# Output sums grown beside their own step's first-matmul turns, with the weights loaded uncast in quarters

## The chip, the cores and the metric

One core of one Trainium2 chip. The metric is the device time of one execution in microseconds (us). All times of a kernel here are the median of its runs. The span of a profile runs from the first to the last instruction and is about 1.7 us shorter than the device time of the same execution. The granted clock is the share of full speed at which TensorE was clocked, as the profile records it.

## The reference, cut to what matters

A short convolution along the sequence with one softmaxed 7-tap filter per head, then a dense block with a Swish of learned slope:

```python
w = softmax(weight)                       # 8 heads x 7 taps
out[b, s, h, :] = sum_k w[h, k] * x_pad[b, s + k, h, :]      # x: 8 x 4096 x 192
h = out.reshape(32768, 192) @ w_in        # 192 -> 2048
g = h / (1 + exp(-beta * h))
return g @ w_out                          # 2048 -> 192, float32
```

## The kernel before

The kernel works in 33 steps: two of 256 tokens, then 31 of 512, each for two halves of the batch at once (rows 0 to 63 and 64 to 127 of the partitions). A step has 16 turns, one for each 128 columns of `w_in`. In a turn TensorE makes the first matmuls (`hidden`), ScalarE turns them into `g`, and TensorE adds to the output sums (`output`) of **the step before**; VectorE copies finished sums out of PSUM (an eviction). "A pair" below is two output matmuls of 192 columns that run together on the two row halves. The convolution of step s+2 is made by VectorE during step s, seven taps in three groups, 21 instructions; for the first two steps TensorE makes it with diagonal matrices.

```python
def hidden(s, fc):
    ...
    ph = psum_h.tile([128, 2, TOK], FP32, name="ph")
    for j in range(NG):                                  # 3
        for h in range(2):                               # the two row halves
            nc.tensor.matmul(ph[:, h, 0:n], w_in_s[rows, j, cols], cts[s][rows, j, 0:n], ...)
    nc.scalar.activation(gs[s][:, fc, :, 0:n], ph[:, :, 0:n], AF.Silu, scale=beta[:, fc : fc + 1])

def output(s, u):                                        # called with s - 1: one step behind
    nb = steps[s][2] // BLK
    per = 2 * nb                                         # 8 pairs a turn in a full step
    for i in range(u * per, (u + 1) * per):
        blk, fc = divmod(i, NF)                          # one block of 128 tokens at a time
        ...
```

The loads. The first chunk (`x0`) has the queue of SyncE to itself. GpSimd's queue, which casts while it loads, brings the first quarter of `w_in`, **then the second chunk (`x1b`)**, then the rest. Only 64 rows of `w_in` are loaded; VectorE copies them to the other 64.

```python
load_x(nc.sync, x0, 0, NB)
...
load_w_in(0)                        # gpsimd, float32 -> bfloat16 in the DMA
for h in range(2):
    nc.gpsimd.dma_start(out=x1b[:, :, h, :], in_=x_v[0, TOK : 2 * TOK, h, :]...)
for i in range(1, NW):
    load_w_in(i)
... # then w_out_raw in four parts, scaled by 1/beta on GpSimd
def copy_w_in(i):
    nc.vector.tensor_copy(w_in_s[DG : 2 * DG, :, cols], w_in_s[0:DG, :, cols])
```

In step 0 the rest of the set-up is hung between the turns. On TensorE it stands in program order, so a late operand stops all that follows (the profile after shows it: 1.6 and 2.9 us):

```python
first_work = {
    0: lambda: (first_xt(), taps()),
    2: lambda: (more(xt1_work)(), copy_w_in(1)),   # transposes of the second chunk
    4: lambda: (more(xt1_work)(), copy_w_in(2)),
    6: lambda: (more(conv1_work)(), copy_w_in(3)), # convolution of step 1 on TensorE
    8: more(conv1_work),
    11: more(conv1_work),
}
```

## Time and profile before

| | before |
|---|---|
| device time, median of 4 runs | 696.3 us |
| span of the profile | 695.1 us |
| TensorE busy | 687.6 us, 99% |
| first first-matmul of step 0 | 10.9 us |
| first full-width activation (start of step 2) | 37.2 us |
| granted clock over the span | 1.000 |

First the head of the profile page: the span, and busy time with its share, engine by engine (PE is TensorE, DVE VectorE, ACT ScalarE, POOL GpSimd).

```profile
span 695.1 us, 24865 instructions
...
PE 687.6 (99%) x11467; PEld 526.6 (76%) x11467; DVE 551.4 (79%) x938; ACT 580.0 (83%) x546; POOL 70.0 (10%) x83
```

TensorE is the bound. Now its timeline near the end (start, length, engine, line, operation, output and inputs, shapes, count). L395 is the first matmuls, L442 the output sums:

```profile
676.21 0.83 PE L395 MATMUL ph<-ct,w_in_s 64*128 64x512 bf16 x6
...
677.51 0.83 PE L395 MATMUL ph<-ct,w_in_s 64*128 64x512 bf16 x6
...
678.82 0.83 PE L395 MATMUL ph<-ct,w_in_s 64*128 64x512 bf16 x6
```

A turn is 1.31 us, with no wait named. The Trainium skill, page "TensorE: Matmul & The Clock Gate", section "Wait — 56ns, not 53.3ns?", gives N/2.4 + 2.5 ns for a matmul of N columns at full clock; the estimate from it for this stream is 3 x (512/2.4 + 2.5) + 8 x (192/2.4 + 2.5) = 1307 ns, and the trace agrees. Only the start and the end can move.

The table of stretches for 12 to 28 us, in step 0 and the beginning of step 1. Columns: the stretch, its length, busy time of TensorE, its weight loads, VectorE, ScalarE and GpSimd, each with a count, then the granted clock, the DMA share and GB/s.

```profile
core 0: us, PE busy (x) PEld busy (x) DVE busy (x) ACT busy (x) POOL busy (x), PEclk, DMA share, GB/s
12.00:16.00 4.00, 3.93 (x70) 2.94 (x65) 2.27 (x6) 3.02 (x5) 0.94 (x1) 1.00 1.09 277
16.00:20.00 4.00, 3.86 (x42) 2.77 (x40) 3.94 (x4) 2.68 (x5) 3.78 (x3) 1.00 1.71 239
20.00:24.00 4.00, 3.09 (x41) 2.30 (x37) 4.00 (x5) 2.91 (x5) 4.00 (x4) 1.00 0.57 57
24.00:28.00 4.00, 3.73 (x74) 3.28 (x71) 4.00 (x7) 3.98 (x7) 4.00 (x6) 1.00 2.03 180
```

The timelines of single engines in the same part: GpSimd's issue of the second chunk (L176), TensorE at its transposes (L243 with `x1b`), VectorE's copies of the last two weight quarters (L172) and the beginning of the convolution for step 2 (L376), and ScalarE's first full-width activations (L402).

```profile
3.72 1.66 POOL L176 DMA_DIRECT2D x1b<-in_x_dram  x2
```

```profile
12.95 0.83 PE L395 MATMUL ph<-ct,w_in_s 64*128 64x256 bf16 x12
13.71 0.47 PE L243 MATMUL po<-ident_b,x1b 128*64 128x128 bf16 x10
```

```profile
16.80 3.04 DVE L172 COPY w_in_s<-w_in_s 64x1536 bf16<-64x1536 bf16 x2
19.88 2.65 DVE L376 TENSOR_SCALAR ct<-xt,cw 128x512 bf16<-128x512 bf16 x2
```

```profile
37.18 18.64 ACT L402 ACTIVATE g<-ph,beta 128x1024 bf16<-128x1024 f32 x18 [1.02 <-PE ph L395]
```

The second chunk is issued at 3.7 us, was there when TensorE came to it at 13.7, and step 2 begins at 37.2. In brackets stands idle time and what ended it.

### The profile page before, as it was taken

How to read it: one execution, taken by the hardware profiler on the slowest of the kernel's cores; microseconds unless marked ns; L12 is line 12 of the kernel's file. 1: busy time of each engine (PE TensorE's matmuls, PEld its weight loads, DVE VectorE, ACT ScalarE, POOL GpSimd, SP SyncE). 2: the span in 40 equal slices, each digit the busy share in tenths (PEclk: the TensorE clock that was granted, in tenths of full speed). 3: DMA queues.
4: the chain of work that ended last, by engine and by line, in shares of the span. 5: the costliest groups of instructions: out<-in, count | busy, mean ns of one | idle time of the engine just before them, and what ended most of it. 6: DMA issues, size and time to landing. Idle time of an engine off the chain costs nothing.

```text
span 695.1 us, 24865 instructions
## 1 busy us (share of the span) xinstructions
PE 687.6 (99%) x11467; PEld 526.6 (76%) x11467; DVE 551.4 (79%) x938; ACT 580.0 (83%) x546; POOL 70.0 (10%) x83
## 2 busy tenths in 40 slices
PE   9999999999999999999999999999999999999997
PEld 6867777777777777777777777777777777777777
DVE  5999998998777987777987777987778987777222
ACT  6898888888888888888888888888888888888881
POOL 7934455000000000000000000000000000000000
PEclk9999999999999999999999999999999999999999
DMA  9999999922232022222023222032222122211012
GB/s 193 144 159 159 168 177 171 123 63 70 54 65 71 27 68 72 47 70 70 26 71 70 49 70 70 25 71 70 48 71 55 40 70 71 48 48 48 25 48 70
DMA packets 181497, 54.57 MB, mean 79 GB/s; under 512 B 146432, under 2 KB 181072, under 8 KB 181392
## 3 DMA queue, kind: packets, MB, share of 16 engines
q0 software_dynamic: 98048, 14.89, 29.8%
q1 hardware_dynamic: 83296, 38.09, 23.9%
q8 instruction: 89, 1.46, 0.9%
q14 instruction: 16, 0.13, 0.1%
q10 hardware_dynamic: 48, 0.01, 0.0%
HBM read 28.98 MB, written 37.29 MB: 95 GB/s over the span
## 4 chain that ended last, share of the span: by engine, by line
PE 96%; DVE 3%; ACT 0%; issue 0%
PE po L442 48%; PE ph L395 46%; DVE ct L378 2%; PE ph L256 0%; DVE w_in_s L172 0%; DVE ct L376 0%; PE ph L205 0%; PE po L209 0%; PE po L243 0%; ACT g L402 0%; PE po L256 0%; DVE xt L346 0%; DVE osb L457 0%; DVE ct L327 0%; ACT xt_145 L269 0%
## 5 line engine op out<-in xcount | busy, mean ns | idle before, releaser
L402 ACT ACTIVATE g<-ph,beta 128x1024 bf16<-128x1024 f32 (+1 forms) x528 | 572.7, 1090 | 96.7 <-PE ph L395 92.6
L442 PEld LDWEIGHTS <-g 64*128 64x128 bf16 x8192 | 369.2, 94 | 101.9
L442 PE MATMUL po<-w_out_s,g 64*128 64x192 bf16 x8192 | 429.8, 243 | 0.0
L395 PE MATMUL ph<-ct,w_in_s 64*128 64x512 bf16 (+1 forms) x3168 | 426.2, 370 | 2.0 <-ACT g L402 1.1
L378 DVE SCALAR_TENSOR_TENSOR ct<-xt,cw,ct 128x512 bf16<-128x512 bf16 x558 | 379.4, 745 | 0.0
L395 PEld LDWEIGHTS <-w_in_s 64*128 64x128 bf16 x3168 | 162.5, 94 | 56.4 <-issue 2.9
L456 DVE COPY osb<-po 128x384 f32<-128x384 f32 x127 | 70.8, 558 | 126.9 <-PE po L442 120.7
L457 DVE TENSOR_TENSOR osb<-po,osb 128x384 f32<-128x384 f32 x129 | 71.5, 555 | 6.0 <-ACT osb L454 1.6
L95 POOL DMA_DIRECT2D xd<-in_x_dram x60 | 54.4, 909 | 46.1 <-DMA xd<-in_x_dram 42.3
L376 DVE TENSOR_SCALAR ct<-xt,cw 128x512 bf16<-128x512 bf16 x93 | 29.5, 372 | 0.0
L454 ACT COPY osb<-po 128x192 f32<-128x192 f32 x2 | 0.6, 320 | 9.9 <-PE po L442 9.9
L352 POOL TENSOR_TENSOR w_out_s<-w_out_raw,beta_r 128x768 bf16<-128x768 f32 x4 | 6.2, 1568 | 2.5 <-DMA w_out_raw<-in_moe_w_out_dram 2.5
L205 PE MATMUL ph<-zeros 128*128 128x512 bf16 x7 | 3.5, 623 | 1.3 <-DVE warm L129 1.3
L172 DVE COPY w_in_s<-w_in_s 64x1536 bf16<-64x1536 bf16 x4 | 4.4, 1121 | 0.1
L256 PE MATMUL po<-xt_145,diag 128*128 128x256 f32 x28 | 4.4, 296 | 0.0
L256 PEld LDWEIGHTS po<-xt_145,diag 128*128 128x128 f32 x28 | 3.6, 189 | 0.7 <-issue 0.6
L256 PEld LDWEIGHTS ph<-xt_145,diag 128*128 128x128 f32 x14 | 3.1, 327 | 0.6 <-ACT xt_145 L269 0.6
L256 PE MATMUL ph<-xt_145,diag 128*128 128x256 f32 x14 | 3.4, 427 | 0.1
L185 POOL DMA_DIRECT2D w_out_raw<-in_moe_w_out_dram x4 | 3.1, 771 | 0.3 <-DMA x1b<-in_x_dram 0.3
L295 ACT ACTIVATE ct<-po,rn 128x256 bf16<-128x256 f32 x1 | 0.5, 475 | 2.6 <-PE po L256 2.6
L165 POOL DMA_DIRECT2D w_in_s<-in_moe_w_in_dram x4 | 2.7, 669 | 0.0
L205 PEld LDWEIGHTS <-zeros 128*128 128x128 bf16 x7 | 0.8, 126 | 2.3 <-DVE warm L129 1.3
(51 smaller groups left out, 28.1 us busy)
## 6 DMA issues: line engine op xcount, KB each, us to landing
out_dram<-osb SPq DMA_DIRECT2D x60, 384.0 KB, 3.1
xd<-in_x_dram POOLq DMA_DIRECT2D x54, 198.0 KB, 14.5
w_out_raw<-in_moe_w_out_dram POOLq DMA_DIRECT2D x4, 384.0 KB, 9.4
out_dram<-osb SPq DMA_DIRECT2D x7, 192.0 KB, 3.7
xd<-in_x_dram POOLq DMA_DIRECT2D x6, 192.0 KB, 13.7
x_83<-in_x_dram SPq DMA_DIRECT2D x4, 192.0 KB, 2.9
w_in_s<-in_moe_w_in_dram POOLq DMA_DIRECT2D x4, 192.0 KB, 7.7
xt<-xd SPq DMA_TRANSPOSE x30, 5.1
```

The source lines that it names most:

```text
L95: nc.gpsimd.dma_start(out=xd[r0:, :, h, :], in_=x_v[p, t0:t1, h, :].rearrange("t (c d) -> t c d", c=NG),)
L172: nc.vector.tensor_copy(w_in_s[DG : 2 * DG, :, cols], w_in_s[0:DG, :, cols])
L205: nc.tensor.matmul(pf[:, 0, :], zeros[:, 0:128], zeros, start=True, stop=True)
L256: nc.tensor.matmul(pv, diag[:, c, k, :], xt0[:, c, o : o + n], start=(k == 0), stop=(k == K - 1),)
L352: nc.gpsimd.tensor_tensor(w_out_s[:, c0 : c0 + n, :], w_out_raw[:, c0 : c0 + n, :], beta_r[:, c0 : c0 + n].unsqueeze(2).to_broadcast((128, ...
L376: nc.vector.tensor_scalar_mul(dst, src, scalar)
L378: nc.vector.scalar_tensor_tensor(out=dst, in0=src, scalar=scalar, in1=dst, op0=ALU.mult, op1=ALU.add)
L395: nc.tensor.matmul(ph[:, h, 0:n], w_in_s[rows, j, cols], cts[s][rows, j, 0:n], start=(j == 0), stop=(j == NG - 1),)
L402: nc.scalar.activation(gs[s][:, fc, :, 0:n], ph[:, :, 0:n], AF.Silu, scale=beta[:, fc : fc + 1])
L442: nc.tensor.matmul(po[:, r, b * D : (b + 1) * D], g[rows, fc, h, q * BLK : (q + 1) * BLK], w_out_s[rows, fc, :], start=(fc == 0), stop=(fc ...
L456: nc.vector.tensor_copy(dst, po[:, 0, cols])
L457: nc.vector.tensor_tensor(dst, po[:, 1, cols], dst, ALU.add)
```

## The change

Intent: let the output sums of a step begin two turns behind its own first matmuls, so that the early steps, in which ScalarE sets the pace and TensorE has room, take some of the output work; the lag then grows over steps 0 to 4. Two blocks of 128 tokens are summed in turn in one PSUM tile. And load all weights as they are (32 bit, by the plain DMA queue), in quarters, to be cast and crossed by GpSimd and VectorE. The core of the diff, cuts marked:

```diff
-    psum_o = ... bufs=2
+    psum_a = ... bufs=1 ;  psum_b = ... bufs=1
 ...
-    load_x(nc.sync, x0, 0, NB)
+    for b in range(HB):
+        load_x0(b)                  # all on nc.sync
+    load_w_in(0)
+    load_w_out(0)
+    for b in range(HB, NB):
+        load_x0(b)
+    for i in range(1, NW):
+        load_w_in(i)
+        load_w_out(i)
 ...
+    cross_w_in(0)                   # VectorE: 2 copies of 64 x 768, 32 bit -> 16
+    cast_w_in(0)                    # GpSimd: waits for the DMA
+    for h in range(2):
+        load_x1(h)                  # GpSimd: the second chunk
+    scale_w_out(0)
+    for i in range(1, NW):
+        cast_w_in(i)
+        scale_w_out(i)
 ...
+    class Job: ...                  # two blocks, 32 pairs, in slot "a" or "b"
+        def ready(self, s, u):
+            fcs = NF if self.s < s else max(0, u - LAG + 1)
+            return self.done < fcs * self.nb
 ...
-        0: lambda: (first_xt(), taps()),
-        2: lambda: (more(xt1_work)(), copy_w_in(1)),
-        4: lambda: (more(xt1_work)(), copy_w_in(2)),
-        6: lambda: (more(conv1_work)(), copy_w_in(3)),
+        0: lambda: (first_xt(), cross_w_in(1)),
+        2: more(xt1_work),
+        3: lambda: cross_w_in(2),
+        4: more(xt1_work),
+        6: more(conv1_work),
+        7: lambda: cross_w_in(3),
 ...
-    pops = {1: 12, 2: 26}
+    quota = {0: 2, 1: 4, 2: 6, 3: 6, 4: 7}       # pairs a turn; 8 from step 5
+    pops = {0: 8, 1: 14, 2: 26}
 ...
-            if s > 0:
-                output(s - 1, u)
+            output(s, u, quota.get(s, 8), "a" if s == 0 else "ab")
```

The taps are also normalised at once, which saves three small matmuls in step 0. Finished sums are stored two blocks at a time, from six buffers in place of three.

More of the change, by code (lines that the diff above doesn't have):

```diff
@@ L67 @@
     g_pool = ctx.enter_context(tc.tile_pool(name="g", bufs=2))
-    osb_pool = ctx.enter_context(tc.tile_pool(name="osb", bufs=3))
+    osb_pool = ctx.enter_context(tc.tile_pool(name="osb", bufs=6))
     psum_h = ctx.enter_context(
@@ L71, with in_a, in_b @@
     )
-    psum_o = ctx.enter_context(
-        tc.tile_pool(name="psum_o", bufs=2, space=bass.MemoryType.PSUM)
+    psum_a = ctx.enter_context(
+        tc.tile_pool(name="psum_a", bufs=1, space=bass.MemoryType.PSUM)
+    )
+    psum_b = ctx.enter_context(
+        tc.tile_pool(name="psum_b", bufs=1, space=bass.MemoryType.PSUM)
     )
     ctx.enter_context(tc.manual_schedule())
+    def in_a():
+        return psum_a.tile([128, 2, TOK], FP32, name="pa")
+    def in_b():
+        return psum_b.tile([128, 2, TOK], FP32, name="pb")
     xds, xts = {}, {}
@@ L113, with load_x0, load_w_in, load_w_out @@
     x1b = setup.tile([128, NB, 2, D], BF16)
-    def load_x(eng, dst, t0, nb):
-        for b in range(nb):
-            t = t0 + b * BLK
-            eng.dma_start(out=dst[:, b, :, :], in_=x_v[0, t : t + BLK, :, :])
+    NW = 4
+    FW = F // NW
+    FH = FW // 2
+    NQ = NF // NW
+    w_in_s = consts.tile([128, NG, F], BF16)
+    w_in_raw = setup.tile([128, NG, NW, FH], FP32)
+    w_out_s = consts.tile([128, NF, D], BF16)
+    w_out_raw = setup.tile([128, NF, D], FP32)
+    w_in_v = moe_w_in.rearrange("(c d) (i r f) -> i r d c f", c=NG, r=2, f=FH)
+    w_out_v = moe_w_out.rearrange("(c p) d -> p c d", p=128)
+    def load_x0(b):
+        nc.sync.dma_start(out=x0[:, b, :, :], in_=x_v[0, b * BLK : (b + 1) * BLK, :, :])
+    def load_w_in(i):
+        for r in range(2):
+            nc.sync.dma_start(
+                out=w_in_raw[r * DG : (r + 1) * DG, :, i, :], in_=w_in_v[i, r]
+            )
+    def load_w_out(i):
+        fcs = slice(i * NQ, (i + 1) * NQ)
+        nc.sync.dma_start(out=w_out_raw[:, fcs, :], in_=w_out_v[:, fcs, :])
+    def load_x1(h):
+        nc.gpsimd.dma_start(
+            out=x1b[:, :, h, :],
+            in_=x_v[0, TOK : 2 * TOK, h, :].rearrange("(b q) d -> q b d", q=BLK),
+        )
     e8 = setup.tile([H, K + 1], FP32)
     cw8 = setup.tile([H, K], FP32)
+    beta_q = setup.tile([NF, 128], FP32)
     nc.scalar.dma_start(out=cw8, in_=weight)
-    load_x(nc.sync, x0, 0, NB)
+    nc.scalar.dma_start(out=beta_q, in_=moe_beta.rearrange("(c p) -> c p", p=128))
+    for b in range(HB):
[7 more added lines that the diff above has]
+        load_w_out(i)
     zeros = setup.tile([128, TOK], BF16)
@@ L156, with cast_w_in, cross_w_in, w_in_of @@
     make_identity(nc, ident)
-    NW = 4
-    FW = F // NW
-    w_in_s = consts.tile([128, NG, F], BF16)
-    def load_w_in(i):
-        cols = slice(i * FW, (i + 1) * FW)
-        nc.gpsimd.dma_start(
-            out=w_in_s[0:DG, :, cols],
-            in_=moe_w_in[:, cols].rearrange("(c d) f -> d c f", c=NG),
-        )
-    def copy_w_in(i):
-        cols = slice(i * FW, (i + 1) * FW)
-        nc.vector.tensor_copy(w_in_s[DG : 2 * DG, :, cols], w_in_s[0:DG, :, cols])
-    load_w_in(0)
-    for h in range(2):
-        nc.gpsimd.dma_start(
-            out=x1b[:, :, h, :],
-            in_=x_v[0, TOK : 2 * TOK, h, :].rearrange("(b q) d -> q b d", q=BLK),
-        )
-    for i in range(1, NW):
-        load_w_in(i)
-    w_out_raw = setup.tile([128, NF, D], FP32)
-    w_out_v = moe_w_out.rearrange("(c p) d -> p c d", p=128)
-    for c in range(0, NF, 4):
-        nc.gpsimd.dma_start(
-            out=w_out_raw[:, c : c + 4, :], in_=w_out_v[:, c : c + 4, :]
+    def cast_w_in(i):
+        nc.gpsimd.tensor_copy(
+            w_in_s[:, :, i * FW : i * FW + FH], w_in_raw[:, :, i, :]
+        )
+    def cross_w_in(i):
+        for r in range(2):
+            nc.vector.tensor_copy(
+                w_in_s[(1 - r) * DG : (2 - r) * DG, :, i * FW + FH : (i + 1) * FW],
+                w_in_raw[r * DG : (r + 1) * DG, :, i, :],
+            )
+    def w_in_of(h, j, fc):
+        i, at = divmod(fc * 128, FW)
+        r, at = divmod(at, FH)
+        f = i * FW + (r ^ h) * FH + at
+        return w_in_s[h * DG : (h + 1) * DG, j, f : f + 128]
+    beta_r = setup.tile([128, NF], FP32)
+    def scale_w_out(i):
+        fcs = slice(i * NQ, (i + 1) * NQ)
+        nc.gpsimd.tensor_tensor(
+            w_out_s[:, fcs, :],
+            w_out_raw[:, fcs, :],
+            beta_r[:, fcs].unsqueeze(2).to_broadcast((128, NQ, D)),
+            ALU.mult,
         )
@@ L194 @@
     )
-    beta_q = setup.tile([NF, 128], FP32)
-    nc.scalar.dma_start(out=beta_q, in_=moe_beta.rearrange("(c p) -> c p", p=128))
     nc.scalar.activation(warm, warm, AF.Silu)
-    e8r = setup.tile([H, K + 1], FP32R)
-    sel_r = setup.tile([H, NG, 2, DG], FP32R)
-    pc = psum_o.tile([128, 2, TOK], FP32, name="po")
+    ident_b = setup.tile([128, 128], BF16)
+    nc.vector.tensor_copy(ident_b, ident)
     pf = psum_h.tile([128, 2, TOK], FP32, name="ph")
@@ L205, in fill @@
             nc.tensor.matmul(pf[:, 0, :], zeros[:, 0:128], zeros, start=True, stop=True)
-    def spread(dst, sel, e8):
-        for c in range(NG):
-            nc.tensor.matmul(
-                dst[:, c * (K + 1) : (c + 1) * (K + 1)],
-                sel[:, c, :, :].rearrange("i h d -> i (h d)"),
-                e8,
-                start=True,
-                stop=True,
-            )
-    nc.vector.tensor_copy(sel_r, sel)
-    ident_b = setup.tile([128, 128], BF16)
-    nc.vector.tensor_copy(ident_b, ident)
-    nc.vector.tensor_copy(e8r, e8)
-    fill(5)
-    spread(pc[:, 0, :], sel_r, e8r)
-    fill(1)
-    eu = setup.tile([128, NG, K + 1], FP32)
-    nc.vector.tensor_copy(eu.rearrange("p c k -> p (c k)"), pc[:, 0, 0 : NG * (K + 1)])
+    fill(5)
+    pq = in_a()[:, 0, 0 : NG * (K + 1)]
+    for c in range(NG):
+        nc.tensor.matmul(
+            pq[:, c * (K + 1) : (c + 1) * (K + 1)],
+            sel[:, c, :, :].rearrange("i h d -> i (h d)"),
+            e8,
+            start=True,
+            stop=True,
+        )
+    pq = pq.rearrange("p (c k) -> p c k", c=NG)
+    fill(1)
+    nc.vector.tensor_copy(x0b[:, 0], x0[:, 0])
+    rq = setup.tile([128, NG], FP32)
+    nc.vector.reciprocal(rq, pq[:, :, K])
+    cw = consts.tile([128, NG, K], FP32)
+    nc.vector.tensor_tensor(
+        cw, pq[:, :, 0:K], rq.unsqueeze(2).to_broadcast((128, NG, K)), ALU.mult
+    )
+    nc.vector.tensor_copy(x0b[:, 1], x0[:, 1])
     diag = setup.tile([128, NG, K, 128], FP32R)
@@ L234, in diag_v @@
             ident.unsqueeze(1).to_broadcast((128, K, 128)),
-            eu[:, c, 0:K].unsqueeze(2).to_broadcast((128, K, 128)),
+            cw[:, c, :].unsqueeze(2).to_broadcast((128, K, 128)),
             ALU.mult,
@@ L265 @@
     for b in range(HB):
-        nc.vector.tensor_copy(x0b[:, b], x0[:, b])
-        pt = psum_o.tile([128, NG, BLK], BF16, name="po")
+        pool, name = (psum_b, "pb") if b == 0 else (psum_a, "pa")
+        pt = pool.tile([128, NG, BLK], BF16, name=name)
         transposes(pt, x0b, b, 0, 1)
         nc.scalar.copy(xt0[:, :, HALO + b * BLK : HALO + (b + 1) * BLK], pt)
+    pb = in_b()[:, 0, 0:NF]
+    nc.tensor.transpose(pb, beta_q, ident[0:NF, 0:NF])
     fill(1)
     diag_v(0)
-    rn = setup.tile([128, NG], FP32)
@@ L273 @@
-    nc.vector.reciprocal(rn, eu[:, :, K])
     diag_v(1)
+    beta = consts.tile([128, NF], FP32)
+    nc.vector.tensor_copy(beta, pb)
+    nc.vector.reciprocal(beta_r, beta)
     for k in range(K):
-        nc.scalar.mul(diag[:, 2, k, :], ident, eu[:, 2, k : k + 1])
+        nc.scalar.mul(diag[:, 2, k, :], ident, cw[:, 2, k : k + 1])
+    cross_w_in(0)
[6 more added lines that the diff above has]
+        scale_w_out(i)
@@ L277 @@
     ct = ct_pool.tile([128, NG, TOK], BF16, name="ct")
     cts[0] = ct
-    pvs = []
     for c in range(NG):
-        pool, name = (psum_h, "ph") if c < 2 else (psum_o, "po")
-        pv = pool.tile([128, 2, TOK], FP32, name=name)[:, 0, 0:n0]
+        pv = psum_h.tile([128, 2, TOK], FP32, name="ph") if c < 2 else in_a()
+        pv = pv[:, 0, 0:n0]
         for k in range(K):
             diag_tap(0, c, k, pv)
-        if c == 0:
-            nc.vector.tensor_scalar_mul(ct[:, c, 0:n0], pv, rn[:, c : c + 1])
-            copy_w_in(0)
-        elif c == 1:
-            nc.vector.tensor_scalar_mul(ct[:, c, 0:n0], pv, rn[:, c : c + 1])
-            pb = psum_o.tile([128, 2, TOK], FP32, name="po")[:, 0, 0:NF]
-            nc.tensor.transpose(pb, beta_q, ident[0:NF, 0:NF])
-            beta = consts.tile([128, NF], FP32)
-            nc.vector.tensor_copy(beta, pb)
-        else:
-            nc.scalar.mul(ct[:, c, 0:n0], pv, rn[:, c : c + 1])
@@ L296 @@
-    beta_r = setup.tile([128, NF], FP32)
-    nc.vector.reciprocal(beta_r, beta)
+        if c < 2:
+            nc.vector.tensor_copy(ct[:, c, 0:n0], pv)
+        else:
+            nc.scalar.copy(ct[:, c, 0:n0], pv)
     nc.vector.tensor_copy(x0b[:, HB:NB], x0[:, HB:NB])
-    cw = consts.tile([128, NG, K], FP32)
-    def taps():
-        pq = psum_o.tile([128, 2, TOK], FP32, name="po")[:, 0, 0 : NG * (K + 1)]
-        spread(pq, sel, e8)
-        pq = pq.rearrange("p (c k) -> p c k", c=NG)
-        rq = setup.tile([128, NG], FP32)
-        nc.vector.reciprocal(rq, pq[:, :, K])
-        nc.vector.tensor_tensor(
-            cw, pq[:, :, 0:K], rq.unsqueeze(2).to_broadcast((128, NG, K)), ALU.mult
-        )
@@ L313, in first_xt @@
     def first_xt():
-        pt = psum_o.tile([128, NG, n0], BF16, name="po")
+        pt = psum_b.tile([128, NG, n0], BF16, name="pb")
         transposes(pt, x0b, HB, 0, HB)
@@ L321, in first_conv @@
         cts[1] = ct_pool.tile([128, NG, TOK], BF16, name="ct")
-        pv = psum_o.tile([128, 4, n0], FP32, name="po")
+        pv = psum_b.tile([128, 4, n0], FP32, name="pb")
         for c in range(NG):
@@ L326, in first_conv @@
             if c == NG - 1:
-                nc.vector.tensor_tensor(
-                    cts[1][:, :, 0:n0],
-                    pv[:, 0:NG, :],
-                    rn.unsqueeze(2).to_broadcast((128, NG, n0)),
-                    ALU.mult,
-                )
+                nc.vector.tensor_copy(cts[1][:, :, 0:n0], pv[:, 0:NG, :])
             yield
@@ L336, in second_xt @@
         xt = new_xt(1)
-        pt = psum_o.tile([128, NG, TOK], BF16, name="po")
+        pt = psum_b.tile([128, NG, TOK], BF16, name="pb")
         for b in range(NB):
@@ L347, in second_xt @@
             yield
-    w_out_s = consts.tile([128, NF, D], BF16)
-    def prep_w_out(c0, n):
-        nc.gpsimd.tensor_tensor(
-            w_out_s[:, c0 : c0 + n, :],
-            w_out_raw[:, c0 : c0 + n, :],
-            beta_r[:, c0 : c0 + n].unsqueeze(2).to_broadcast((128, n, D)),
-            ALU.mult,
-        )
     cast(2)
-    for c in range(0, NF, 4):
-        prep_w_out(c, 4)
     cast(3)
@@ L390, in hidden @@
         ph = psum_h.tile([128, 2, TOK], FP32, name="ph")
-        cols = slice(fc * 128, (fc + 1) * 128)
         for j in range(NG):
@@ L396, in hidden @@
                     ph[:, h, 0:n],
-                    w_in_s[rows, j, cols],
+                    w_in_of(h, j, fc),
                     cts[s][rows, j, 0:n],
@@ L404, in hidden, with __init__, pair @@
         )
-    state = {}
-    def store(s, h, q, n_q, osb):
-        ch, t0, n = steps[s]
-        p, c = divmod(ch, CHUNKS)
-        if s < N_ST - 1:
-            if q < n // BLK - 1:
-                return
-            n_q = n // BLK
-        t = c * TOK + t0 + (q + 1 - n_q) * BLK
-        nc.sync.dma_start(
-            out=out_v[h, p, t : t + n_q * BLK, :].rearrange("(b q) d -> q b d", q=BLK),
-            in_=osb[:, q + 1 - n_q : q + 1, :],
-        )
-    def output(s, u):
-        g = gs[s]
-        nb = steps[s][2] // BLK
-        per = 2 * nb
-        for i in range(u * per, (u + 1) * per):
-            blk, fc = divmod(i, NF)
-            h, q = divmod(blk, nb)
-            b = q % 2
-            single = s == N_ST - 1 and h == 1 and q >= nb - 2
-            if single:
-                b = 0
-            if fc == 0 and b == 0:
-                state["po"] = psum_o.tile([128, 2, TOK], FP32, name="po")
-            if fc == 0 and q == 0:
-                state["osb"] = osb_pool.tile([128, TOK // BLK, D], FP32, name="osb")
-            po, osb = state["po"], state["osb"]
+    class Job:
+        def __init__(self, s, h, q, nb):
+            self.s, self.h, self.q, self.nb = s, h, q, nb
+            self.done, self.po = 0, None
+        def ready(self, s, u):
+            fcs = NF if self.s < s else max(0, u - LAG + 1)
+            return self.done < fcs * self.nb
+        def pair(self):
+            fc, b = divmod(self.done, self.nb)
+            g = gs[self.s]
+            q = self.q + b
             for r in range(2):
@@ L442, in output @@
                 nc.tensor.matmul(
-                    po[:, r, b * D : (b + 1) * D],
-                    g[rows, fc, h, q * BLK : (q + 1) * BLK],
+                    self.po[:, r, b * D : (b + 1) * D],
+                    g[rows, fc, self.h, q * BLK : (q + 1) * BLK],
                     w_out_s[rows, fc, :],
-                    start=(fc == 0),
+                    start=(self.done == 0),
                     stop=(fc == NF - 1),
+                    skip_group_check=True,
                 )
-            if fc == NF - 1 and (b == 1 or single):
-                n_q = 1 if single else 2
-                cols = slice((b + 1 - n_q) * D, (b + 1) * D)
-                dst = osb[:, q + 1 - n_q : q + 1, :].rearrange("p b d -> p (b d)")
-                if single:
-                    nc.scalar.copy(dst, po[:, 0, cols])
-                else:
-                    nc.vector.tensor_copy(dst, po[:, 0, cols])
-                nc.vector.tensor_tensor(dst, po[:, 1, cols], dst, ALU.add)
-                store(s, h, q, n_q, osb)
+            self.done += 1
@@ new lines, in pair, with leave @@
+            return self.done == NF * self.nb
+        def leave(self):
+            nb = self.nb
+            osb = osb_pool.tile([128, 2, D], FP32, name="osb")
+            dst = osb[:, 0:nb, :].rearrange("p b d -> p (b d)")
+            if nb == 1:
+                nc.scalar.copy(dst, self.po[:, 0, 0 : nb * D])
+            else:
+                nc.vector.tensor_copy(dst, self.po[:, 0, 0 : nb * D])
+            nc.vector.tensor_tensor(dst, self.po[:, 1, 0 : nb * D], dst, ALU.add)
+            ch, t0, n = steps[self.s]
+            p, c = divmod(ch, CHUNKS)
+            t = c * TOK + t0 + self.q * BLK
+            nc.sync.dma_start(
+                out=out_v[self.h, p, t : t + nb * BLK, :].rearrange(
+                    "(b q) d -> q b d", q=BLK
+                ),
+                in_=osb[:, 0:nb, :],
+            )
@@ new lines, with jobs_of, output @@
+    LAG = 2
+    waiting = deque()
+    slots = {"a": None, "b": None}
+    place = {"a": in_a, "b": in_b}
+    def jobs_of(s):
+        nb = steps[s][2] // BLK
+        for h in range(2):
+            for q in range(0, nb, 2):
+                if s == N_ST - 1 and h == 1 and q == nb - 2:
+                    waiting.extend([Job(s, h, q, 1), Job(s, h, q + 1, 1)])
+                else:
+                    waiting.append(Job(s, h, q, 2))
+    def output(s, u, pairs, free):
+        for _ in range(pairs):
+            for name in free:
+                if slots[name] is None and waiting:
+                    slots[name] = waiting.popleft()
+            live = [(j.s, j.h, j.q, n) for n, j in slots.items() if j is not None]
+            for *_, name in sorted(live):
+                job = slots[name]
+                if job.ready(s, u):
+                    break
+            else:
+                return
+            if job.po is None:
+                job.po = place[name]()
+            if job.pair():
+                job.leave()
+                slots[name] = None
@@ L475 @@
     }
-    pops = {1: 12, 2: 26}
+    quota = {0: 2, 1: 4, 2: 6, 3: 6, 4: 7}
+    pops = {0: 8, 1: 14, 2: 26}
     queue = deque()
-    for s in range(N_ST + 1):
+    for s in range(N_ST):
         if s + 2 < N_ST:
             queue.extend(conv_ops(s + 2))
+        jobs_of(s)
         for u in range(NF):
-            if s < N_ST:
-                hidden(s, u)
-            if s > 0:
-                output(s - 1, u)
+            hidden(s, u)
+            output(s, u, quota.get(s, 8), "a" if s == 0 else "ab")
             if s == 0 and u in first_work:
@@ L489 @@
             n = pops.get(s, 24)
-            pops_u = (u + 1) * n // NF - u * n // NF if s else u > 5
+            pops_u = (u + 1) * n // NF - u * n // NF if s else u >= NF - n
             for _ in range(pops_u):
@@ L497 @@
                 xpose(s + 2)
+    while waiting or any(slots.values()):
+        output(N_ST, 0, 1, "ab")
 _INS = ['x', 'weight', 'moe_w_in', 'moe_w_out', 'moe_beta']
```

## The prediction

> **What bounds the kernel now.** TensorE. The page's busy table gives it 687.6 of 695.1 us; the table of stretches shows it 100% busy at granted clock 1.00 from 53.2 us to the last step's end. A steady turn streams, the two row halves together, three first matmuls of 512 columns and eight output matmuls of 192. The Trainium skill, "TensorE: Matmul & The Clock Gate" (section "Wait — 56ns, not 53.3ns?"), gives N/2.4 GHz + 2.5 ns per warm matmul: 3x215.8 + 8x82.5 = 1307 ns. The chain of waits repeats every 1.307 us, so the trace agrees and the steady state has nothing left to give; VectorE (82%) and ScalarE (85%) have slack there. 32 full-step equivalents x 16 x 1.3075 = 669.4 us. Only the other 26 us can move: 10.9 before the first turn, 11 lost in the first three steps (42.3 us for 31.4 us of this work), 4 after the last matmul.
>
> **What the change does.** Outputs are no longer exactly one step behind. The quotas, cut by the lag, place 28+64+96+96+112 pairs in steps 0 to 4; the backlog is then 116 pairs and stays so, against 128 before. Interleaving two blocks in a PSUM tile changes no matmul, weight load or eviction size, and each tile still has four turns (5.2 us) before reuse, against 1.1 us of eviction (two 0.56 us instructions). So no steady loss either.
>
> Gains:
> - 28 pairs (28 x 0.082 = 2.3 us) move into step 0, which takes 14.5 us for 5.3 us of first matmuls, held by set-up work and ScalarE.
> - Step 2 took 16.7 us at ScalarE's pace (1.015 us a turn) for 15.7 us of PE work; with six pairs a turn it is PE-bound (1.14 us): 0.9 us.
> - The second tap spreading (0.8 us of PE) goes.
>
> Costs:
> - GpSimd now issues the second chunk's load behind a weight cast that waits for its DMA: at about 7.3 us instead of 3.7, beside 3.8 MB of plain loads. I estimate landing at 14-16 us against 10-11. The transposes of turn 2 (13.7 us before) stand in PE order and may stall 0.5-2 us.
> - The convolution for step 2 runs from 19.9 to 36.5 us now, just holding step 2. One more eviction pair (1.1 us) enters its queue; weight copies get somewhat cheaper. I put step 2's start 0 to 3 us later.
> - The first DRAM casts move from 10.9 to about 20-22 us; their transposed chunk should be there by 35-37 us, when VectorE first needs it. Narrow.
>
> **Sum.** 4 us of gain (2.3+0.9+0.8) less about 2: 694.2 us, 8 in 10 within 690.5 to 698.5. Faster by over 2%: 0.01; same: 0.96; slower: 0.03.
>
> **What would show each step.** Steady turn 1.307 us; three fewer tap-spread matmuls, else equal counts; clock 1.00. Last stretch of outputs alone 9.5-10 us instead of 11.1. Turns of 1.14 us in steps 2 and 3 (18.3 us each); full-rate turns from step 5, near 92-94 us. Second-chunk load landing at 14-16 us, TensorE idle before its transposes; step-2 convolution ending at 36-39 us.
>
> **What would make it wrong.** Plain loads landing later, or GpSimd's casts much slower beside VectorE's copies: then the second chunk or the first transposed chunk is late, and VectorE, whose queue is in order, holds step 2 or 3 (several us slower). Or the loads land early, step 0 packs tightly and 4 us or more are won. A big surprise needs a steady turn other than 1.307 us, for instance if alternating blocks cost TensorE time: 0.1 us a turn is 45 us.

## The result, and the profile after

| | before | after |
|---|---|---|
| device time, median (range), 4 runs each | 696.3 us (695.9 to 696.8) | 704.7 us (701.9 to 705.5) |
| ratio of the means | | 1.0110, 95% interval 1.0090 to 1.0131 |
| granted clock of those runs | 1.000 (profiled run) | 0.998, 0.994, 0.992, 0.992 |
| span of the profile | 695.1 us | 700.2 us (the 701.9 us run) |
| start of step 2 | 37.2 us | 44.9 us |

A ratio is the mean time of one kernel's runs over that of the other's of the same rounds, so not quite the ratio of the medians.

The kernel is about 8 us (1.1%) slower, outside the predicted range of 690.5 to 698.5 us though within the 2% that the prediction calls "same", and its runs scatter over 3.6 us where those of before lie within 0.9. The profile is of the quickest of the four. Its head and its steady turns (L398 the first matmuls, L426 the outputs):

```profile
span 700.2 us, 25076 instructions
...
PE 688.7 (98%) x11464; PEld 504.6 (72%) x11464; DVE 554.1 (79%) x938; ACT 580.5 (83%) x546; POOL 67.5 (10%) x79
```

```profile
681.03 0.81 PE L398 MATMUL ph<-ct,w_in_s 64*128 64x512 bf16 x6
...
682.34 0.81 PE L398 MATMUL ph<-ct,w_in_s 64*128 64x512 bf16 x6
```

The steady turn is unchanged, 1.31 us. The loss is at the start. The same stretches and engines as before:

```profile
12.00:16.00 4.00, 2.24 (x35) 1.34 (x32) 3.28 (x5) 2.19 (x4) 2.45 (x3) 1.00 1.29 224
16.00:20.00 4.00, 1.25 (x17) 0.95 (x19) 2.54 (x3) 0.00 (x0) 2.27 (x2) 0.78 1.02 226
20.00:24.00 4.00, 4.00 (x57) 3.06 (x53) 1.80 (x2) 2.64 (x4) 3.73 (x5) 0.79 0.25 16
24.00:28.00 4.00, 3.88 (x58) 3.16 (x58) 2.38 (x5) 2.40 (x4) 4.00 (x5) 1.00 2.15 138
```

```profile
6.70 0.83 POOL L202 CAST w_in_s<-w_in_raw 128x768 bf16<-128x768 f32 x1 [3.77 <-DMA w_in_raw<-in_moe_w_in_dram]
7.48 1.67 POOL L150 DMA_DIRECT2D x1b<-in_x_dram  x2
```

```profile
13.71 0.33 PE L426 MATMUL pa<-w_out_s,g 64*128 64x192 bf16 x4
15.59 0.24 PE L279 MATMUL pb<-ident_b,x1b 128*64 128x128 bf16 x1 [1.55 <-DMA x1b<-in_x_dram]
18.75 0.85 PE L279 MATMUL pb<-ident_b,x1b 128*64 128x128 bf16 x11 [2.92 <-DMA x1b<-in_x_dram]
```

```profile
22.17 0.96 DVE L363 COPY xt<-pb 128x1536 bf16<-128x1536 bf16 x1 [3.56 <-PE pb L279]
23.16 1.89 DVE L208 CAST w_in_s<-w_in_raw 64x768 bf16<-64x768 f32 x2
25.08 1.36 DVE L380 TENSOR_SCALAR ct<-xt,cw 128x512 bf16<-128x512 bf16 x3
29.34 0.96 DVE L349 CAST ct<-pb 128x768 bf16<-128x768 f32 x1 [2.90 <-PE pb L292]
```

```profile
44.87 19.13 ACT L405 ACTIVATE g<-ph,beta 128x1024 bf16<-128x1024 f32 x17 [1.89 <-PE ph L398]
```

GpSimd waits 3.8 us for the first weights, casts them, and only then issues the second chunk, at 7.5 us. Its two halves come so late that TensorE idles 1.6 and 2.9 us before its transposes (L279). From 16 to 24 us its clock is 0.78 and 0.79, and in one-microsecond stretches it is 0.50 from 19 to 21 us: it was lowered while TensorE stood still, and the work that then came ran at half rate. VectorE gets the second chunk at 22.2 us instead of 15.8, then stands another 2.9 us before L349, which waits for TensorE. Step 2 begins 7.7 us later. GpSimd's two issuing instructions took no longer than before (1.67 us against 1.66), so what was late is their start and the transfer, not the issue itself.

### The profile page after: what moved, and what is told of

It is laid out like the page before. It is cut to its first block, busy times and chain, and to the rows that moved or that the text cites. A ratio compares the mean times of both kernels' runs of the same rounds, so it can differ in the third digit from the quotient of the medians.

```text
span 700.2 us, 25076 instructions
## 1 busy us (share of the span) xinstructions
PE 688.7 (98%) x11464; PEld 504.6 (72%) x11464; DVE 554.1 (79%) x938; ACT 580.5 (83%) x546; POOL 67.5 (10%) x79
## 4 chain that ended last, share of the span: by engine, by line
PE 94%; DVE 2%; DMA 2%; issue 0%; SPq 0%; ACT 0%; POOL 0%; POOLq 0%
PE ph L398 46%; PE pa L426 24%; PE pb L426 24%; DVE ct L382 2%; DMA x1b<-in_x_dram 1%; DMA w_in_raw<-in_moe_w_in_dram 1%; PE pb L292 0%; DVE osb L445 0%; DVE osb L444 0%; PE pb L279 0%; DVE ct L349 0%; SPq L137 0%; POOL w_in_s L202 0%; SPq L141 0%; ACT g L405 0%
## 5 line engine op out<-in xcount | busy, mean ns | idle before, releaser
L426 PEld LDWEIGHTS <-g 64*128 64x128 bf16 x8192 | 354.2, 94 | 119.6 <-issue 0.8
L398 PE MATMUL ph<-ct,w_in_s 64*128 64x512 bf16 (+1 forms) x3168 | 419.5, 370 | 0.7 <-DVE ct L382 0.3
L426 PE MATMUL pa<-w_out_s,g 64*128 64x192 bf16 x4128 | 217.2, 243 | 0.9 <-issue 0.6
L426 PE MATMUL pb<-w_out_s,g 64*128 64x192 bf16 x4064 | 211.4, 243 | 0.0
L398 PEld LDWEIGHTS <-w_in_s 64*128 64x128 bf16 x3168 | 147.0, 94 | 62.0 <-issue 2.1
L444 DVE COPY osb<-pa 128x384 f32<-128x384 f32 x64 | 35.6, 557 | 99.2 <-PE pa L426 96.2
L444 DVE COPY osb<-pb 128x384 f32<-128x384 f32 x63 | 35.1, 557 | 26.2 <-PE pb L426 20.6
L445 DVE TENSOR_TENSOR osb<-pa,osb 128x384 f32<-128x384 f32 (+1 forms) x65 | 36.0, 554 | 3.3 <-ACT osb L442 1.1
L445 DVE TENSOR_TENSOR osb<-pb,osb 128x384 f32<-128x384 f32 x64 | 35.5, 554 | 2.7 <-ACT osb L442 0.5
L208 DVE CAST w_in_s<-w_in_raw 64x768 bf16<-64x768 f32 x8 | 7.2, 905 | 0.2
L279 PE MATMUL pb<-ident_b,x1b 128*64 128x128 bf16 x24 | 1.7, 270 | 4.5 <-DMA x1b<-in_x_dram 4.5
L279 PEld LDWEIGHTS <-x1b 128*64 128x64 bf16 x24 | 1.1, 140 | 5.1 <-DMA x1b<-in_x_dram 4.8
L363 DVE COPY xt<-pb 128x1536 bf16<-128x1536 bf16 x1 | 1.0, 957 | 3.6 <-PE pb L279 3.6
## 6 DMA issues: line engine op xcount, KB each, us to landing
xd<-in_x_dram POOLq DMA_DIRECT2D x6, 192.0 KB, 15.6
```

The source lines that it names most:

```text
L208: nc.vector.tensor_copy(w_in_s[(1 - r) * DG : (2 - r) * DG, :, i * FW + FH : (i + 1) * FW], w_in_raw[r * DG : (r + 1) * DG, :, i, :],)
L398: nc.tensor.matmul(ph[:, h, 0:n], w_in_of(h, j, fc), cts[s][rows, j, 0:n], start=(j == 0), stop=(j == NG - 1),)
L426: nc.tensor.matmul(self.po[:, r, b * D : (b + 1) * D], g[rows, fc, self.h, q * BLK : (q + 1) * BLK], w_out_s[rows, fc, :], start=(self.don ...
L444: nc.vector.tensor_copy(dst, self.po[:, 0, 0 : nb * D])
L445: nc.vector.tensor_tensor(dst, self.po[:, 1, 0 : nb * D], dst, ALU.add)
```

## The experiments

Thirteen kernels were run, most with five timed runs; all gave correct results. Kernels that were run together share the runs of the kernel before (medians 696.2 to 696.6 us).

One number orders them all. Take from each profile the start of step 2 (ScalarE's first full-width activation) and subtract it from the span:

| run | outputs | start of step 2, us | span, us | rest, us |
|---|---|---|---|---|
| before | one step behind | 37.2 | 695.1 | 657.9 |
| e3_before_x1_late | one step behind | 43.3 | 701.2 | 657.9 |
| e4_x1_early_one_step | one step behind | 43.4 | 701.0 | 657.6 |
| e11_before_copy_twice | one step behind | 39.8 | 697.7 | 657.9 |
| after | new | 44.9 | 700.2 | 655.3 |
| e8_after_again | new | 48.2 | 703.5 | 655.3 |
| e1_x1_early | new | 44.7 | 700.0 | 655.3 |
| e2_fill | new | 44.6 | 699.9 | 655.3 |
| e6_order_x1_early | new | 44.3 | 699.7 | 655.4 |
| e7_order_one_queue | new | 42.2 | 697.2 | 655.0 |
| e9_w_out_last | new | 42.8 | 697.9 | 655.1 |
| e12_cross_later | new | 40.7 | 695.8 | 655.1 |
| e13_cross_half_act | new | 39.8 | 695.0 | 655.2 |
| e5_before_new_out | new | 38.4 | 693.6 | 655.2 |
| e10_new_out_conv_first | new | 37.1 | 693.0 | 656.0 |

The new output order is worth about 2.6 us (2.2 to 2.9) in all that follows the start of step 2, whatever came before it; everything else is when step 2 starts. So the profile after is 7.7 - 2.6 = 5.1 us longer than the profile before, and e8_after_again, a more typical run of the changed kernel, 11.0 - 2.6 = 8.4 us. (The last row is the one exception; it waited 0.9 us for a PSUM tile soon after, see there.)

**e1_x1_early.** The load of the second chunk moved ahead of GpSimd's first wait.

```diff
+    for h in range(2):
+        load_x1(h)          # right after make_identity
 ...
     cast_w_in(0)
-    for h in range(2):
-        load_x1(h)
```

> The changed kernel with one thing undone: the load of the second chunk is issued by GpSimd before it waits for the weights (at about 3 us instead of 7.5), everything else as changed. Theory A (the late second chunk leaves TensorE idle for 4.5 us in turn 2 of step 0, and the idle time then lowers the granted clock): the idle goes, the clock is 1.000 in every run, the repeats agree within 1 us, and the 28 pairs and step 2 pay as predicted: 691 to 694 us. Rival B (the output order itself costs time): still 700 to 705 us. Rival C (the plain loads crowd it out whatever its issue time): it lands 8 to 10 us after its issue, at 11.5 to 13 us, or later; if at 16 us or more, half of the loss stays (697 to 700 us).

Measured: 701.1 us (699.8 to 701.7), ratio to before 1.0064 (1.0050 to 1.0078), clocks 0.995 to 0.997. The loss was not undone. TensorE and VectorE in step 0:

```profile
15.77 0.53 PE L281 MATMUL pb<-ident_b,x0b 128*64 128x128 bf16 x12 [3.94 <-DVE x0b L335]
```

```profile
15.15 0.56 DVE L335 CAST x0b<-x 128x768 bf16<-128x768 f32 x1 [4.21 <-DMA x<-in_x_dram]
```

The second chunk no longer holds anything. Instead the second half of the first chunk, which stands in the plain queue behind 768 KB of weights, lands at 15.1 us (before that it had landed by 11.9) and TensorE idles 3.9 us for that. The second chunk itself took 8.0 to 11.6 us to land, against 5.9 to 6.1 in the kernel before. The Trainium skill, page "DMA: Bandwidth & Descriptors", section "Queues, rings and completion order", says that a DMA engine takes turns between the queues that have work; that two busy queues delayed each other here would fit it, but no run isolated it: the same loads took 6.2 to 8.6 us in e4_x1_early_one_step, and in e3_before_x1_late, behind loads of GpSimd's own queue, 8.3 to 9.6 us. Theory A as first put, one late load, fell; rival C came nearer.

**e2_fill.** Twenty matmuls of zeros before the late transposes, with the wait left in.

```diff
+        pz = in_b()
+        for _ in range(20):
+            nc.tensor.matmul(pz[:, 0, :], zeros[:, 0:128], zeros, start=True, stop=True)
         pt = psum_b.tile([128, NG, TOK], BF16, name="pb")
```

> The changed kernel with 20 matmuls of zeros (about 4.3 us) ahead of the late transposes, so that TensorE is busy while it waits; the wait stays. It separates the clock from the wait. If the spread of 702 to 705.5 us and the clocks of 0.992 to 0.998 come from the idle stretch: clock 1.000 in all runs, repeats within 1 us, 698 to 700.5 us. If the clock falls for another reason: still 702 to 705.5 us with clocks below 0.999.

Measured: 701.9 us (700.7 to 703.4), clock 1.000 in all five runs.

```profile
16.00:20.00 4.00, 3.40 (x23) 1.50 (x23) 2.93 (x4) 0.00 (x0) 1.64 (x2) 1.00 0.94 206
20.00:24.00 4.00, 4.00 (x72) 3.19 (x68) 2.05 (x3) 2.53 (x4) 4.00 (x4) 1.00 0.01 2
```

So the idle stretch is what lowers the clock, as expected; the time is 1.4 us above the expected range; in the profile the second half of the chunk landed at 19.8 us, a microsecond later than in the changed kernel's. The scatter of 2.7 us that is left is not the clock's; the landing of the load is its likely cause, but only one run of each set has a trace. Against the changed kernel (704.7 and 705.1 us in its two sets, other rounds) the clock is worth 2 to 3 us: about 3 by the medians, about 2 by the ratios to the kernel before (1.0082 against 1.0110 and 1.0116).

**e3_before_x1_late.** The kernel before, with the second chunk issued after all weights.

> The kernel before with one thing done: the second chunk's load is issued after all weight loads on the same queue, so that it lands at about 16 to 18 us. Theory A: TensorE idles 2 to 4 us before those transposes, the clock falls below 1 in some or all runs, and the time rises by 4 to 10 us to 700 to 706 us, without any of the new output order. Rival B: under 2 us of rise (696 to 698 us).

Measured: 703.0 us, ratio 1.0098 (1.0084 to 1.0112), clock 0.995 in every run; TensorE waited 5.4 us for the chunk:

```profile
18.20 0.32 PE L243 MATMUL po<-ident_b,x1b 128*64 128x128 bf16 x1 [4.66 <-DMA x1b<-in_x_dram]
19.30 0.84 PE L243 MATMUL po<-ident_b,x1b 128*64 128x128 bf16 x11 [0.78 <-DMA x1b<-in_x_dram]
```

A late second chunk alone, with no new output order, costs 6.8 us, most of the 8.4 us of the whole change. A late chunk is enough for a loss of this kind, but e1_x1_early shows that it is not all of it.

**e4_x1_early_one_step.** As e1_x1_early, with `ready` and `quota` set so that outputs are one step behind again.

> As the first of these runs (early second chunk), but outputs again exactly one step behind (no pairs in step 0, 4 a turn in steps 1 and 2, 8 after). It gives the worth of the growing beside the own step alone. By the prediction it is worth 2.3 us for the 28 pairs of step 0 and 0.9 us for step 2: 2 to 4 us slower than the first run, 694 to 697 us. Rival B (the new order costs time): faster than the first run.

Measured: 702.6 us (1.5 us slower than e1_x1_early; 2 to 4 were expected). Step 2 started 1.2 us earlier, the rest took 2.3 us longer: that makes the 1.0 us between the two spans. The worth of the order is in the rest. What happened ahead of step 2 is not a clean comparison: the loads are the same as in e1_x1_early, but here the first chunk's second half cost TensorE 1.3 us instead of 3.9, and then it waited 3.4 us for VectorE's copy of the second chunk (L363), which stood behind four weight copies, as later in e9_w_out_last. So the landing of the same loads varies from run to run.

**e5_before_new_out.** The kernel before with its own loads, and only the new output order (the pairs of step 0 in turns 8 to 15).

> The kernel before, with its loads and set-up untouched, and only the new output order (jobs of two blocks, lag 2, backlog built up over steps 0 to 4; the pairs of step 0 are placed in turns 8 to 15, as its output weights are ready only near 18 us). If the loads alone cost the time (theory A, widened: the plain loads bring the second chunk or the second half of the first chunk late): 692 to 695.5 us, clock 1.000. If the output order costs time (rival B): 697 us or more.

Measured: 695.3 us, ratio 0.9981 (0.9966 to 0.9996), clocks 0.999 to 1.000. The new output order gains 1.3 us and rival B is out: step 2 starts 1.2 us later, for the added pairs and evictions, and 2.6 us come back.

**e6_order_x1_early** and **e7_order_one_queue.** The first chunk's four blocks first, then each quarter of `w_out` a place later; in the second of the two, the second chunk too goes by the plain queue, in its place, and is cast by GpSimd.

```diff
     for b in range(HB, NB):
         load_x0(b)
+    # e7: the second chunk here, 4 loads, on nc.sync
     for i in range(1, NW):
         load_w_in(i)
-        load_w_out(i)
+        load_w_out(i - 1)
+    load_w_out(NW - 1)
```

> The changed kernel with another order of its loads: the four blocks of the first chunk and the first quarter of the first weights first, then each quarter of the output weights one place later; the second chunk's load early on GpSimd's queue, as in the first run of the study. In that run the second half of the first chunk came at 15.1 us instead of 11.9, because it stood behind 768 KB of weights and shared the DMA engines with the second chunk. If order is the cause: the idle in front of its transposes goes, the idle before the second chunk is under 2 us, 694 to 698 us. If the sheer volume in the first 20 us is the cause whatever its order: 699 us or more.

> As the run before it, but the second chunk is loaded as 32-bit numbers by the same queue as all else, in the place where it is wanted, and cast by GpSimd, so that nothing shares the engines with it. If it is the sharing of the engines between two queues that delays both: the second chunk lands by 10 to 11 us and is cast by 13 us, no TensorE idle over 1 us in step 0, clock 1.000, 691.5 to 695.5 us. If the volume is the cause: 698 us or more.

Measured: 700.2 us (clocks 0.994 to 1.000) and 699.1 us (0.997 to 1.000). In both the wait for the chunks is gone, and TensorE waits for the output weights instead, 3.4 and 2.7 us. From the second:

```profile
16.66 0.34 PE L431 MATMUL pa<-w_out_s,g 64*128 64x192 bf16 x4 [2.73 <-POOL w_out_s L228]
```

Growing the sums beside their own step needs `w_out` in turn 2 of step 0, about 12 us earlier than before, while the load of everything goes on until about 20 us. Both missed the lower expected ranges and fell in those for "volume". But e12_cross_later below, with the same volume, came back to 696.9 us, so the volume by itself does not explain the time.

**e8_after_again.** The changed kernel, unedited.

> The changed kernel unedited, on the same chip as the three above, for its spread and its clocks: 702 to 705.5 us, clocks 0.992 to 0.998 as before; below 700 us in a run would mean that the late load is itself a matter of chance.

Measured: 705.1 us (703.5 to 705.6), clocks 0.992 to 0.995. Its profile, a slow example, has the second chunk's halves at 17.5 and 20.8 us and the clock low for ten microseconds:

```profile
16.00:20.00 4.00, 0.31 (x1) 0.12 (x1) 3.60 (x5) 0.00 (x0) 2.19 (x2) 0.54 1.17 237
20.00:24.00 4.00, 3.16 (x39) 2.28 (x41) 0.00 (x0) 1.24 (x2) 3.19 (x3) 0.50 0.07 18
24.00:28.00 4.00, 4.00 (x47) 2.99 (x45) 3.37 (x6) 1.51 (x3) 4.00 (x6) 0.68 1.71 109
```

**e9_w_out_last.** As e7_order_one_queue, with all of `w_out` loaded last and the pairs of step 0 in turns 8 to 15, four each.

> As the one-queue run, with the output weights loaded after all first weights, and the pairs of step 0 placed in turns 8 to 15, so that TensorE waits neither for the second chunk nor for the output weights (the one-queue run waited 2.9 us for those). If those two waits and the clock are all of the loss: 694.5 to 696 us, as the run that had the old loads and the new output order (695.3). If VectorE's chain to step 2 is also longer by the dearer weight copies (7.2 us busy in the changed kernel against 4.4 in the kernel before): 696.5 to 698.5 us with clock 1.000 and TensorE waiting for the convolution of step 2.

Measured: 700.1 us (698.3 to 701.8), clocks 0.994 to 0.998. No gain, outside both ranges: neither load is late now, and TensorE waits for VectorE. TensorE, then VectorE, then the stretch after the wait:

```profile
13.77 0.53 PE L284 MATMUL pb<-ident_b,x1b 128*64 128x128 bf16 x12 [0.29 <-DVE xt L345]
...
19.21 1.09 PE L297 MATMUL pb<-xt,diag 128*128 128x256 f32 x7 [2.62 <-DVE xt L368]
```

```profile
13.75 3.39 DVE L213 CAST w_in_s<-w_in_raw 64x768 bf16<-64x768 f32 x4
17.17 1.13 DVE L365 CAST xt<-xt 128x18 bf16<-128x18 f32 x1
18.22 0.94 DVE L368 COPY xt<-pb 128x1536 bf16<-128x1536 bf16 x1
```

```profile
20.00:24.00 4.00, 4.00 (x34) 3.06 (x34) 3.94 (x5) 1.27 (x2) 3.79 (x3) 0.59 0.02 4
```

The transposes are made at 13.8 us as in the kernel before, but VectorE, in order, first makes four weight copies (3.4 us) and comes to the chunk (L368) at 18.2. The next convolution on TensorE (L297) writes to the same tile: the change split the two interchangeable PSUM tiles into `pa` and `pb`, and in step 0 all set-up work uses `pb` (read from the code; no run put the two tiles back). So TensorE waits 2.6 us, and the clock falls to 0.59.

**e10_new_out_conv_first.** As e5_before_new_out, with the convolution for step 2 queued ahead of step 1's second eviction.

> The old loads with the new output order, and in step 1 all of the convolution for step 2 queued on VectorE ahead of that step's second eviction. In the run without this, TensorE waited for that convolution until 38.0 us, and one eviction (1.1 us) stood before its end. If VectorE's queue sets the start of step 2: about 1 us faster, 693.8 to 694.8 us. If not: no change, 695 to 695.6 us.

Measured: 695.1 us, ratio 0.9978 (0.9966 to 0.9991), against 695.3: no real change. The wait moved: step 2 started 1.3 us sooner, then TensorE waited 0.9 us for the PSUM tile whose eviction had been put back. It and e5_before_new_out are the versions that beat both kernels, by a little.

**e11_before_copy_twice.** The kernel before, each weight copy made twice.

> The kernel before with each of its four weight copies on VectorE done twice (same result): 2.8 to 4.4 us more work on VectorE ahead of the convolution for step 2, nothing else. If VectorE's chain to step 2 is critical one for one: 698.5 to 701 us. If there is slack in it: under 697 us.

Measured: 699.5 us, ratio 1.0037 (1.0025 to 1.0049). Three microseconds for about 4 us more work, but not all of it is VectorE's queue: TensorE waited 1.9 us for the copies once, and the clock fell with it in three of five runs (0.996 to 0.998).

```profile
20.51 0.50 PE L396 MATMUL ph<-ct,w_in_s 64*128 64x256 bf16 x5 [1.90 <-DVE w_in_s L173]
```

The two runs at 0.999 and 1.000 were 1.4 and 1.9 us over the kernel before, the other three 2.9 to 3.5. So VectorE's queue ahead of the convolution for step 2 has little slack, but one for one is not shown.

**e12_cross_later** and **e13_cross_half_act.** As e9_w_out_last, with the third weight copy behind the second chunk's copy; in the second also half of the last three copies on ScalarE.

```diff
-        3: lambda: cross_w_in(2),
         4: more(xt1_work),
+        5: lambda: cross_w_in(2),
 ...
+            # e13 only
+            copy = nc.scalar.copy if i > 0 and r == 1 else nc.vector.tensor_copy
```

> As the run with the output weights last, with the third weight copy moved from turn 3 to turn 5, behind the second chunk's copy. There VectorE did that copy first, the second chunk's copy came at 18.2 us, and TensorE waited 2.6 us for the one PSUM tile that both share with the next convolution; the clock fell again. If that order in VectorE's queue is the cause of what is left: TensorE idle in step 0 under 1 us, clock 1.000 (at least 0.999), 696 to 698 us. The rest against 695.3 would be the longer chain of VectorE. If the clock still falls or the time stays at 699 or more, the cause is another.

> As the run beside it, with one half of each of the last three weight copies given to ScalarE (about 2.4 us less on VectorE ahead of the convolution for step 2). If VectorE's chain with the dearer copies is the rest of the loss: step 2 starts 1 to 2.5 us earlier than in the run beside it and the time falls by as much, to 694.5 to 696.5 us. If ScalarE's own extra work holds step 0 instead: no gain.

Measured: 696.9 us (clocks 0.999 to 1.000), ratio 1.0005 (0.9993 to 1.0017); and 696.5 us, ratio 1.0001 (0.9989 to 1.0013). In the first, TensorE and the clock in the stretches that were bad before:

```profile
17.48 1.09 PE L297 MATMUL pb<-xt,diag 128*128 128x256 f32 x7 [0.32 <-DVE xt L368]
```

```profile
16.00:20.00 4.00, 3.68 (x53) 2.75 (x48) 3.91 (x5) 2.82 (x5) 3.64 (x4) 1.00 0.95 277
20.00:24.00 4.00, 4.00 (x60) 3.46 (x61) 3.90 (x4) 2.31 (x4) 4.00 (x3) 1.00 0.02 4
```

One copy moved by two turns took 3.2 us off (medians, two sets of rounds): the wait of 2.6 us, now 0.3, and the low clock after it. With it the 8 us of loss are gone while the weights are still loaded uncast. The 0.5 us between the two medians are within the noise (the intervals overlap, and the second kernel's runs go from 696.0 to 698.5 us). In its profile the convolution for step 2 ended and step 2 started 0.9 us sooner, just short of the 1 to 2.5 us expected, since its copies on VectorE still ran long.

## Why the prediction was wrong

- **The steady state: right.** 1.31 us a turn before and after, and no cost of alternating blocks. The rest after the start of step 2 is constant to 0.4 us in ten of the eleven profiles with the new order.
- **The gain of the output order: right in kind.** The 2.3 us of pairs and 0.9 us of step 2, 3.2 us together, measured about 2.6 us (2.2 to 2.9 over the pairs of kernels). Alone on the old loads it made 1.3 us net.
- **The step that failed: "I put step 2's start 0 to 3 us later."** It was 7.7 us later in one profile and 11.0 in the other. Its parts:
  - "I estimate landing at 14-16 us" and "may stall 0.5-2 us": the two halves landed at 15.6 and 18.7 us (17.5 and 20.8 in the second profile), and the stalls were 4.5 and 6.5 us. The prediction had the issue time right (7.5 us against 7.3), but allowed 7 to 9 us from issue to landing, little more than the 6 us of the kernel before. In the two profiles of the changed kernel, beside 3.8 MB of plain loads, it was 8.1 to 12.4 us. e3_before_x1_late shows that such a stall costs 7 us by itself.
  - **Nothing was put down for the clock.** The prediction said 1.00. In eight of the profiles (after, e1, e3, e4, e6, e8, e9, e11) such waits lowered TensorE's clock to one half for 3 to 10 us, in the stretch in which the lost time should have been made good. Filling the wait with matmuls (e2_fill) put it back to 1.000 in all runs and saved 2 to 3 us.
  - "Weight copies get somewhat cheaper": they were 7.2 us on VectorE against 4.4. As many elements in all, but read as 32-bit numbers, and more of them beside GpSimd's casts: one copy takes 0.69 us when it is alone and up to 1.6 us beside a GpSimd instruction. The Trainium skill, page "GPSIMD Engine Reference", section "2. Architecture", says that GpSimd's ports to SBUF are shared with VectorE; the durations fit, but no run isolated it. That this queue has little slack, e11_before_copy_twice showed.
- **Under "what would make it wrong" stood** late plain loads and slow casts, "several us slower": the direction was seen, but the range reached only to 698.5 us.
- **My own first theory fell too.** The late second chunk was one of four things that stood in a row: take it away, and the second half of the first chunk was late; put the loads in order, and the output weights were; put those last, and VectorE's copies stood before the chunk's. Only with all four mended (e12_cross_later) did the time come back to 696.9 us.
- **What is left:** 1.6 us between e12_cross_later and e5_before_new_out. In their profiles all of the difference lies before step 2 (40.7 against 38.4 us; the rest is 655.1 and 655.2 us), where VectorE ended its weight copies at 23.7 against 19.3 us. The transposed chunk for step 3, for which VectorE waited 0.5 and 0.9 us in the last two runs, comes after the convolution for step 2, so it had no part in this. **Open** is why the copies slow down beside GpSimd, and what makes the landing times vary from run to run.

## What to carry to other kernels

In a start-up phase ask for each load not only when it is issued but what else is in flight, and write down in what order the operands are wanted; work that is moved earlier pulls its operands forward too. When engines run in order and hand work to each other, removing the wait you see only shows the next one, so follow a fixed mark (here the start of step 2) rather than a single wait. And price a wait of TensorE at more than its length: here two to six idle microseconds were in most profiles followed by several at half clock.

## What the Trainium skill lacked or had wrong

- "TensorE: Matmul & The Clock Gate" (its closing table and "HAM oscillation") warns of idle gaps above about 3 or 3.4 us. Here 2.6 us (e9_w_out_last) and 1.9 us (e11_before_copy_twice) of idle time, with thin work around it, were enough to bring the clock to 0.50, while 2.7 us in e7_order_one_queue left it at 1.00: the length of the gap alone did not decide.
- For when the clock falls after work stops, the same page ("Seeing it yourself") has one measured case, 5.2 us after the last matmul. Here short stretches show the fall 2.3 to 4.8 us after the idle time began (14.0 to 18.3 us in the changed kernel's first profile, 14.0 to 16.3 in the second, 11.8 to 16.6 in e1_x1_early), and in e1_x1_early, e9_w_out_last and e11_before_copy_twice after TensorE had already resumed.
- "DMA: Bandwidth & Descriptors" gives turns between queues but no figure for what a busy plain queue does to a casting one: the same two loads of 192 KB (as written) took 5.3 to 6.1 us to land in the kernels with the old loads (before, e5, e10), and 6.1 to 12.4 us beside plain weight loads (after, e1, e2, e4, e6, e8). The queue is not the only thing that counts: issued last on GpSimd's own queue (e3_before_x1_late), they took 8.3 to 9.6 us.
